# Moving the gate multiplication of a fused attention and mixture kernel from one phase to the input of the next

## The chip, the cores and the metric

One core of one Trainium2 chip runs the whole program in one launch. The metric is the device time of one execution in microseconds (us); lower is better. Engine names are those of the profile: PE is TensorE (its matmuls), PEld its weight loads, DVE is VectorE, ACT is ScalarE, POOL is GpSimd, SP is the engine that only issues transfers here. A queue name with a q (ACTq, SPq) is the instruction stream of an engine as an issuer of transfers.

## The reference

Three layers in a row, in 32-bit floats, for 8 batches of 576 tokens and a model width of 512:

```python
kv  = einsum('bhsd,bhse->bhde', k, v);  out = einsum('bhsd,bhde->bhse', q, kv)   # linear attention, 8 heads of 64
x   = out / sqrt(mean(out^2) + 1e-6) * g_norm
xk, xr = mu_k*x + (1-mu_k)*x_prev,  mu_r*x + (1-mu_r)*x_prev                     # x_prev: one token earlier
v   = relu(xk @ w_k)^2 @ w_v                                                     # 512 -> 1024 -> 512
r   = sigmoid(xr @ w_r)
x2  = r * v                                                                      # the gate multiplication
# then, with x2: 4 experts of causal softmax attention (64 wide), the 2 best of 4 by a router, w_o
```

## The kernel before

All matrices are kept transposed: 128 partitions hold features, the free dimension holds tokens. A 32-bit product is made of three single-pass matmuls: each operand is split into a high part (an ACT copy with rounding) and a low part (a subtraction on DVE or POOL), and `mm3` (lines 74 to 78) adds high by high, high by low and low by high. `split` (lines 70 to 72) is the pair of instructions.

**Stages.** `phase_a` computes the attention, r and relu(.)^2 for all batches; it stores r to the DRAM tensors `sgd` and the squares to `kkd`. `phase_v` (the w_v phase, lines 663 to 760) does the product with w_v, batch by batch, by a seven-product block scheme (`BLOCKS`); the two outer halves of a batch's input (tile `kin`) are subtracted from each other (tiles `tv`, two buffers) and split (tiles `kk`, five buffers) by `prep` (lines 150 to 179), one batch ahead of the products. `phase2` (lines 761 to 1084) does the expert attention.

**The gate in the w_v phase.** `load_s` (lines 144 to 148) loads a batch's r from `sgd` into tiles `sgv`. `gated` (lines 688 to 692) takes one finished quarter: DVE adds or subtracts two terms into a tile `ct` (three buffers), and POOL multiplies `ct` into `sgv` in place. There are eight quarters of 128 x 288 a batch. Two stores on the SP queue (lines 717 and 728) send the gated half batches to the DRAM tensors `x2d`.

**Second-phase weights.** `weights2` (lines 80 to 123) loads and splits the weights of the second phase while the w_v phase runs. The first 256 columns of `w_qk` are scaled by -1/8: a DVE instruction scales the staged tile `wst` in place (line 101), then `split` runs over all 512 columns.

**Second-phase input.** In the second phase a batch has two halves `HF`, tokens 0 to 255 and 256 to 575. `prep(b, hf)` (lines 772 to 787) loads x2 of one half into the tile `x2in` (one buffer, issued on the ACT queue, line 779) and then, in four pieces, rounds it on ACT (line 785) and subtracts on POOL (line 786). For batch 0 it is different: in the last w_v batch (lines 739 to 755) both halves of batch 0 are loaded, and the first half is split there, a piece at a time, between the products; the second half is split at the start of the second phase, with two of its four subtractions on DVE.

**Order of work.** The second phase is software-pipelined by steps `g`: scores, exponentials (`expo`, line 912), normalization on POOL (`norm`, line 929) one step later, transposes on PE (`transp`, line 949) four steps later. There are 18 steps a batch. The next batch's two `prep` generators start at steps `P0` and `P1` and advance by one piece a step; projections of the next batch (`fill_n`) are spread from step `CUT` on. The instructions are written in this order, but outside phase_a a planner (`schedule_with_timeline_sim=True`) sets the order on each engine from its own simulated times: an instruction that is ready in the simulation may go ahead of others written before it on the same engine. `tc.keep_in_program_order` ties an instruction behind the one written before it on its engine. On the chip each engine then runs its list strictly in order, and an instruction that waits holds up all behind it.

Two PSUM tiles `acc` (`AB = 2`) are shared by all projections of the second phase, so the third projection can't start before the first one has been copied out by ACT and DVE.

Of the kernel before, what the change touches and what calls it, by code (L numbers as in the profile page):

```python
# [9 lines left out]
F32 = mybir.dt.float32  # L10
F32R = mybir.dt.float32r
# [4 lines left out]
ALU = mybir.AluOpType  # L16
# [9 lines left out]
def tile_kernel(ctx: ExitStack, tc: tile.TileContext, qT, kv, par, w_r, w_k, w_v, w_qk, w_vg, w_o, out):  # L26
# [53 lines left out]
    def weights2():  # L80
# [16 lines left out]
        def load_w(wh, wl, w, kt, f, scaled=0):  # L97
            st = w2.tile([P, DM], F32, name="wst", bufs=2)
            nc.sync.dma_start(st[:, :f], w[kt * P:(kt + 1) * P, :])
            if scaled:  # L100
                nc.vector.tensor_scalar(st[:, :scaled], st[:, :scaled], -D ** -0.5, None, op0=ALU.mult)
            split(wh[:, kt, :], wl[:, kt, :], st[:, :f])

# [30 lines left out]

    kin, ops, sgt = {}, {}, {}

    def load(b):
        if b < B:
            for h in range(2):
                for i in range(2):  # L140
                    kin[b, i, h] = W["sv"].tile([P, KH, HS], F32, name="kin", bufs=5)
                    nc.sync.dma_start(kin[b, i, h], kkd[b][:, KH * i:KH * i + KH, h * HS:(h + 1) * HS])

    def load_s(b):
        if b < B:
            for i in range(2):
                sgt[b, i] = W["sv"].tile([P, KD // 2, S], F32, name="sgv", bufs=3)
                nc.sync.dma_start(sgt[b, i], sgd[b][:, 2 * i:2 * i + 2, :])

# [513 lines left out]
    def phase_v():  # L663
        with ExitStack():
            sb = W["sv"]

            def products(b):
# [19 lines left out]

                def gated(i, m, h, op, x, y):
                    c = sb.tile([P, HS], F32, name="ct", bufs=3)
                    op(c, x, y)  # L690
                    g = sgt[b, i][:, m, h * HS:(h + 1) * HS]
                    nc.gpsimd.tensor_mul(g, c, g)  # L692
                add, sub = nc.vector.tensor_add, nc.vector.tensor_sub
# [6 lines left out]
                for m in MM:  # L700
                    q = bank()
                    prod(q, "a12", "b21", m, True, True)
                    gated(0, m, 0, add, q[:, :HS], p1[m])
                yield
# [9 lines left out]
                for m in MM:  # L714
                    prod(qd[m], "s4", "b22", m, False, True)
                    gated(0, m, 1, add, qd[m][:, :HS], u2[m])
                nc.sync.dma_start(x2d[b][:, :2, :], sgt[b, 0])
                yield
# [4 lines left out]
                for m in MM:  # L723
                    prod(qa[m], "s3", "t3", m, False, True)
                    u3 = kept(qa[m], "vu")
                    gated(1, m, 1, add, qa[m][:, :HS], p5[m])
                    gated(1, m, 0, sub, u3, qc[m][:, :HS])
                nc.sync.dma_start(x2d[b][:, 2:, :], sgt[b, 1])
                yield

            load_s(0)
            load(1)
            for b in range(B):
                if b > 0:
                    load(b + 1)
                load_s(b + 1)
                if b == 2:
                    w2 = weights2()
                if b == B - 1:
                    for _ in w2:  # L740
                        pass
                    W["x2"] = ExitStack()
                    x2p = W["x2"].enter_context(tc.tile_pool(name="x2p", bufs=1, reuse_waits="tile"))
                    x21 = W["x21"] = x2p.tile([P, KD, S - 256], F32, name="x21")
                    x2, xh, xl = W["x20"] = [x2p.tile([P, KD, 256], t, name=f"x20{u}") for t, u in ((F32, "i"), (F32R, "h"), (F32R, "l"))]
                    nc.sync.dma_start(x2, x2d[0][:, :, :256])
                    nc.sync.dma_start(x21, x2d[0][:, :, 256:])
                pr = prep(b + 1) if b + 1 < B else None
                for n, _ in enumerate(products(b)):
# [3 lines left out]
                    if b == B - 1 and 0 < n < 5:  # L753
                        nc.scalar.activation(xh[:, n - 1, :], x2[:, n - 1, :], AF.Copy)
                        nc.gpsimd.tensor_sub(xl[:, n - 1, :], x2[:, n - 1, :], xh[:, n - 1, :].bitcast(F32))
                for _ in pr or ():
# [4 lines left out]
    def phase2():  # L761
        with ExitStack() as st2:
# [9 lines left out]
            def prep(b, hf):  # L772
                q0, q1 = HF[hf]
                w = q1 - q0
                if b == 0:
                    x2 = W["x21"]
                else:
                    x2 = sb.tile([P, KD, HW], F32, name="x2in", bufs=1)
                    nc.scalar.dma_start(x2[:, :, :w], x2d[b][:, :, q0:q1])
                xh = sb.tile([P, KD, w], F32R, name=f"x2h{hf}", bufs=1)  # L780
# [3 lines left out]
                for i in range(KD):  # L784
                    nc.scalar.activation(xh[:, i, :], x2[:, i, :w], AF.Copy)
                    (nc.gpsimd if b or i % 2 else nc.vector).tensor_sub(xl[:, i, :], x2[:, i, :w], xh[:, i, :].bitcast(F32))  # L786
                    yield
# [227 lines left out]

            x2t[0, 0] = W["x20"][1:]
            for _ in prep(0, 1):
                pass
            for f in fill_n(0):
# [4 lines left out]
            Z0, Z1 = 9, 11  # L1024
            P0, P1 = 3, 9
            L1, L2, L3, L4, L5, L6 = 2, 8, 9, 22, 13, 22
# [32 lines left out]
            for g in range(NG + 2 * NC):  # L1059
                b, s = divmod(g, NS)  # L1060
                if b + 1 < B:
                    if s == P0 + (b == 0):
                        pn = prep(b + 1, 0)
                    if s == P1:
                        pn = prep(b + 1, 1)
                    next(pn, None)
# [61 lines left out]
```

## Time and profile before

| | |
|---|---|
| median of 3 runs | 991.35 us (990.33 to 991.79) |
| the profiled execution's own time | 991.67 us |
| its span (first to last instruction) | 989.9 us |
| mean granted clock of PE | 0.989 of full |
| PE busy | 949.4 us (96%) |
| PEld busy | 870.1 us (88%) |
| DVE busy | 651.5 us (66%) |
| ACT busy | 536.3 us (54%) |
| POOL busy | 427.0 us (43%) |

Read it so: the stages follow each other in time on all engines. phase_a runs to about 390 us, the w_v phase from there to 604 us, the second phase from 604 us to the end. A busy share of PE near 100% in a stretch means that matmuls follow each other without a gap that the profile shows; only a stretch below that has time to give back. The time of an execution is 1.8 us more than its span.

### The profile page before, as it was taken

To read this page: it belongs to the slowest core of one execution; us is meant where nothing else is said; L and a number is where in the kernel's file an instruction comes from. 1 tells how busy PE (TensorE), PEld (TensorE's weight loads), DVE (VectorE), ACT (ScalarE), POOL (GpSimd) and SP (SyncE) were. 2 spreads that over 40 slices of the span, in tenths; PEclk is the share of its full clock that TensorE was granted. 3 is DMA by queue.
4 is the path that set the end of the run, shared out by engine and by line. 5 is a ranking of instruction groups with operands and counts; after the bars stand their busy time and mean duration, and the time that the engine had idled before them with its cause. 6 is when DMAs were issued, how large, how long until landed. Compare 5 with 4: busy or idle time off the path is not lost.

```text
span 989.9 us, 20990 instructions
## 1 busy us (share of the span) xinstructions
PE 949.4 (96%) x7912; PEld 870.1 (88%) x7912; DVE 651.5 (66%) x1537; ACT 536.3 (54%) x1320; POOL 427.0 (43%) x516
## 2 busy tenths in 40 slices
PE   5779999999999999999999998999999999999998
PEld 2669899989899999999999997988988888888986
DVE  4897675867576763579987883665556565656553
ACT  4664765756666665455454543546354546455454
POOL 0025052433253422657888885427152433435231
PEclk9789999999999999999999999999999999999999
DMA  9752737363546224866666623002030202120102
GB/s 345 228 162 91 226 106 237 110 222 123 199 147 196 74 79 117 294 196 223 220 217 210 208 104 116 22 6 97 1 97 2 96 27 71 28 71 27 49 13 85
DMA packets 74901, 127.20 MB, mean 129 GB/s; under 512 B 6448, under 2 KB 57136, under 8 KB 74800
## 3 DMA queue, kind: packets, MB, share of 16 engines
q1 hardware_dynamic: 57760, 104.10, 31.4%
q10 hardware_dynamic: 17040, 21.77, 7.0%
q8 instruction: 62, 1.02, 0.4%
q14 instruction: 39, 0.32, 0.1%
HBM read 78.66 MB, written 47.19 MB: 127 GB/s over the span
## 4 chain that ended last, share of the span: by engine, by line
PE 76%; DVE 7%; ACT 7%; DMA 5%; POOL 3%; issue 2%; ACTq 0%; DVEq 0%; POOLq 0%
PE acc L76 16%; PE acc L77 15%; PE acc L78 15%; PE qa L680 6%; PE qd L680 4%; PE acc L680 4%; DMA x2in<-x2d 3%; PE acc L976 3%; PE pt L949 3%; PE s L900 2%; ACT pr L912 2%; POOL x2l L786 2%; PE acc L300 2%; POOL pr L929 1%; PE po L316 1%
## 5 line engine op out<-in xcount | busy, mean ns | idle before, releaser
L437 POOL TENSOR_TENSOR ksq<-rl 128x288 f32<-128x288 f32 x128 | 99.5, 783 | 148.2 <-ACT rl L435 142.7
L77 PE MATMUL acc<-mixl,wkh 128*128 128x288 f32 x512 | 154.3, 302 | 0.2 <-DVE mixl L66 0.2
L76 PE MATMUL acc<-mixh,wkh 128*128 128x288 f32 x512 | 151.1, 299 | 3.4 <-ACT mixh L409 2.8
L78 PE MATMUL acc<-mixh,wkl 128*128 128x288 f32 x512 | 151.3, 296 | 0.0
L912 ACT ACTIVATE pr<-pr,nm 128x256 f32<-128x256 f32 (+4 forms) x144 | 83.2, 579 | 73.3 <-DVE nm L866 72.4
L929 POOL TENSOR_SCALAR pr<-pr,rc,wg 128x512 f32<-128x512 f32 (+3 forms) x128 | 76.2, 608 | 104.0 <-DVE wg L859 62.4
L76 PEld LDWEIGHTS acc<-mixh,wkh 128*128 128x128 f32 x512 | 96.3, 190 | 4.6 <-ACT mixh L409 3.3
L77 PEld LDWEIGHTS acc<-mixl,wkh 128*128 128x128 f32 x512 | 97.1, 190 | 2.2 <-DVE mixl L66 0.4
L692 POOL TENSOR_TENSOR sgv<-ct,sgv 128x288 f32<-128x288 f32 x64 | 82.5, 1313 | 35.2 <-DVE ct L690 34.7
L78 PEld LDWEIGHTS acc<-mixh,wkl 128*128 128x128 f32 x512 | 97.4, 190 | 0.0
L403 DVE TENSOR_TENSOR mixl<-xm,mixh 128x288 fp32r<-128x288 f32 x116 | 58.3, 538 | 52.3 <-ACT mixh L409 52.3
L435 ACT ACTIVATE rl<-acc 128x288 f32<-128x288 f32 x128 | 51.6, 405 | 71.5 <-PE acc L78 52.7
L866 DVE CUSTOM_DVE_ANT_0 pr<-s,mask 128x256 f32<-128x256 f32 (+4 forms) x144 | 66.9, 481 | 17.2 <-PE pt L949 12.8
L76 PE MATMUL acc<-x2h,wqh 128*128 128x320 f32 (+1 forms) x240 | 74.5, 311 | 3.5 <-DVE vs L829 3.5
L76 PE MATMUL acc<-mixh,wrh 128*128 128x288 f32 x240 | 74.6, 311 | 0.6 <-ACT sg L66 0.6
L408 DVE SCALAR_TENSOR_TENSOR xm<-xT,pars,xm 128x288 f32<-128x288 f32 x116 | 69.0, 624 | 5.1 <-ACT xm L400 5.0
L78 PE MATMUL acc<-x2h,wql 128*128 128x320 f32 (+1 forms) x240 | 71.2, 297 | 0.0
L400 ACT ACTIVATE xm<-xT,nus 128x288 f32<-128x288 f32 x120 | 61.0, 532 | 18.8 <-DVE mixl L403 9.2
L77 PE MATMUL acc<-x2l,wqh 128*128 128x320 f32 (+1 forms) x240 | 71.1, 296 | 0.0
L78 PE MATMUL acc<-mixh,wrl 128*128 128x288 f32 x240 | 71.0, 296 | 0.0
L77 PE MATMUL acc<-mixl,wrh 128*128 128x288 f32 x240 | 70.4, 293 | 0.0
L72 DVE TENSOR_TENSOR kk<-tv,kk 128x1152 fp32r<-128x1152 f32 x32 | 59.8, 1886 | 7.3 <-ACT kk L71 7.3
(239 smaller groups left out, 2753.4 us busy)
## 6 DMA issues: line engine op xcount, KB each, us to landing
kkd<-ksq SPq DMA_DIRECT2D x128, 144.0 KB, 1.8
kin<-kkd SPq DMA_DIRECT2D x32, 576.0 KB, 4.6
kvt<-in_kv SPq DMA_DIRECT2D x24, 512.0 KB, 5.7
qt<-in_qT SPq DMA_DIRECT2D x16, 576.0 KB, 7.0
sgv<-sgd SPq DMA_DIRECT2D x16, 576.0 KB, 3.8
x2d<-sgv SPq DMA_DIRECT2D x16, 576.0 KB, 2.9
sgd<-sg ACTq DMA_DIRECT2D x56, 144.0 KB, 3.7
out<-ob SPq DMA_DIRECT2D x28, 288.0 KB, 2.1
```

The costliest lines, as they stand in the source:

```text
L72: vec.tensor_sub(lo, src, hi.bitcast(F32))
L76: ten.matmul(ps, wh(i), xh(i), start=(i == 0), stop=False)
L77: ten.matmul(ps, wh(i), xl(i), start=False, stop=False)
L78: ten.matmul(ps, wl(i), xh(i), start=False, stop=(i == n - 1))
L400: act.activation(xs[p], xT[:, p, h * HS:(h + 1) * HS], AF.Copy, scale=nu[:, p:p + 1])
L408: vec.scalar_tensor_tensor(xs[p], xT[:, p, cols(h)], mu[:, p:p + 1], xs[p], op0=ALU.mult, op1=ALU.add)
L437: nc.gpsimd.tensor_mul(sq, rl, rl)
L680: nc.tensor.matmul(q[:, :HS], a[:, i, ms_], c[:, i, :], start=(start and i == 0 and n == 0), stop=(stop and i == KH - 1 and n == 2), skip_ ...
L692: nc.gpsimd.tensor_mul(g, c, g)
L866: nc.vector.tensor_tensor_reduce(out=pr[:R, k0:k0 + kn], in0=s[:R, :kn], in1=mk, scale=1.0, scalar=lo, op0=ALU.add, op1=ALU.min, accum_out ...
L912: nc.scalar.activation(pr[:, :L], pr[:, :L], AF.Exp, bias=nm, scale=-1.0, accum_out=sms[b, p, j][:, e2:e2 + 1])
L929: nc.gpsimd.tensor_scalar(pr[:, :L], pr[:, :L], rc[:, r:r + 1], wg, op0=ALU.mult, op1=ALU.mult)
```

## The change

- `gated` becomes `put`: DVE writes each finished quarter straight into an output tile `vo` (three buffers of a half batch); the POOL multiplication, the tile `ct` and the loads of `sgd` in the w_v phase go. `x2d` then holds v, not r * v.
- In the last w_v batch both halves of batch 0 are loaded in four parts, each with its part of r; the loads reuse the buffers `kin` and `tv`. After each of the products 1 to 4, one part is multiplied on POOL, rounded on ACT and subtracted on POOL. The second phase starts with batch 0 split whole.
- `prep` of the second phase loads x2 and r (tile `gin`), two buffers each, on the SP queue. Each piece is multiplied on POOL in place, rounded on ACT (now tied in program order) and subtracted on POOL.
- `P1` is 8 and not 9, and what is left of the first half's generator is run out before the second starts.
- The scaled columns of `w_qk` are rounded by ACT with the scale inside, and DVE makes the low part in one instruction with the scale inside.

```diff
         def load_w(wh, wl, w, kt, f, scaled=0):
...
             if scaled:
-                nc.vector.tensor_scalar(st[:, :scaled], st[:, :scaled], -D ** -0.5, None, op0=ALU.mult)
-            split(wh[:, kt, :], wl[:, kt, :], st[:, :f])
+                nc.scalar.activation(h[:, :scaled], st[:, :scaled], AF.Copy, scale=-D ** -0.5)
+                nc.vector.scalar_tensor_tensor(l[:, :scaled], st[:, :scaled], -D ** -0.5, h[:, :scaled].bitcast(F32), op0=ALU.mult, op1=ALU.subtract)
+            split(h[:, scaled:], l[:, scaled:], st[:, scaled:f])
...
-                def gated(i, m, h, op, x, y):
-                    c = sb.tile([P, HS], F32, name="ct", bufs=3)
-                    op(c, x, y)
-                    g = sgt[b, i][:, m, h * HS:(h + 1) * HS]
-                    nc.gpsimd.tensor_mul(g, c, g)
+                out_ = [sb.tile([P, KD // 2, S], F32, name="vo", bufs=3) for _ in range(2)]
+
+                def put(i, m, h, op, x, y):
+                    op(out_[i][:, m, h * HS:(h + 1) * HS], x, y)
...
-                nc.sync.dma_start(x2d[b][:, :2, :], sgt[b, 0])
+                nc.sync.dma_start(x2d[b][:, :2, :], out_[0])
...
-                load_s(b + 1)
...
-                    x21 = W["x21"] = x2p.tile([P, KD, S - 256], F32, name="x21")
-                    x2, xh, xl = W["x20"] = [x2p.tile([P, KD, 256], t, name=f"x20{u}") for t, u in ((F32, "i"), (F32R, "h"), (F32R, "l"))]
-                    nc.sync.dma_start(x2, x2d[0][:, :, :256])
-                    nc.sync.dma_start(x21, x2d[0][:, :, 256:])
+                    cuts = [(0, 256), (256, S)]
+                    W["x2t"] = [[x2p.tile([P, KD, c1 - c0], F32R, name=f"x2{i}{u}") for u in "hl"] for i, (c0, c1) in enumerate(cuts)]
+                    parts = []
+                    for (c0, c1), hl in zip(cuts, W["x2t"]):
+                        for i in range(0, KD, 2):
+                            raw = []
+                            for name, src, n in (("kin", x2d, 5), ("tv", sgd, 2)):
+                                t = sb.tile([P, KH, HS], F32, name=name, bufs=n).rearrange("p k t -> p (k t)")[:, :2 * (c1 - c0)]
+                                raw.append(t.rearrange("p (k t) -> p k t", k=2))
+                                nc.sync.dma_start(raw[-1], src[0][:, i:i + 2, c0:c1])
+                            parts.append([x[:, i:i + 2, :] for x in hl] + raw)
...
                     if b == B - 1 and 0 < n < 5:
-                        nc.scalar.activation(xh[:, n - 1, :], x2[:, n - 1, :], AF.Copy)
-                        nc.gpsimd.tensor_sub(xl[:, n - 1, :], x2[:, n - 1, :], xh[:, n - 1, :].bitcast(F32))
+                        h, l, x, g = parts[n - 1]
+                        nc.gpsimd.tensor_mul(x, x, g)
+                        act.activation(h, x, AF.Copy)
+                        nc.gpsimd.tensor_sub(l, x, h.bitcast(F32))
...
-                if b == 0:
-                    x2 = W["x21"]
-                else:
-                    x2 = sb.tile([P, KD, HW], F32, name="x2in", bufs=1)
-                    nc.scalar.dma_start(x2[:, :, :w], x2d[b][:, :, q0:q1])
+                x2, g = [sb.tile([P, KD, HW], F32, name=name, bufs=2) for name in ("x2in", "gin")]
+                for t, src in ((x2, x2d), (g, sgd)):
+                    nc.sync.dma_start(t[:, :, :w], src[b][:, :, q0:q1])
...
-                    nc.scalar.activation(xh[:, i, :], x2[:, i, :w], AF.Copy)
-                    (nc.gpsimd if b or i % 2 else nc.vector).tensor_sub(xl[:, i, :], x2[:, i, :w], xh[:, i, :].bitcast(F32))
+                    x = x2[:, i, :w]
+                    nc.gpsimd.tensor_mul(x, x, g[:, i, :w])
+                    tc.keep_in_program_order(nc.scalar.activation(xh[:, i, :], x, AF.Copy))
+                    nc.gpsimd.tensor_sub(xl[:, i, :], x, xh[:, i, :].bitcast(F32))
...
-            for _ in prep(0, 1):
-                pass
...
-            P0, P1 = 3, 9
+            P0, P1 = 3, 8
...
                     if s == P1:
+                        for _ in pn:
+                            pass
                         pn = prep(b + 1, 1)
```

## Rows read from the trace of the kernel before

**Rows 1.** Stretches: start:end, length, busy PE PEld DVE ACT POOL, PEclk, DMA, GB/s.
```profile
440.00:450.00 10.00, 8.49 (x64) 8.20 (x63) 10.00 (x10) 4.66 (x10) 8.45 (x4) 1.00 0.69 199
...
480.00:600.00 120.00, 120.00 (x892) 118.78 (x891) 99.14 (x89) 54.00 (x76) 95.77 (x55) 1.00 0.55 184
...
615.00:625.00 10.00, 6.53 (x39) 6.36 (x40) 2.28 (x9) 3.90 (x11) 0.74 (x3) 0.83 0.23 67
...
650.00:930.00 280.00, 276.06 (x2228) 244.96 (x2228) 165.17 (x619) 145.53 (x454) 114.94 (x190) 1.00 0.15 50
```

**Rows 2.** Waits of PE, whole span: waiter <- releaser: us in total, times, longest.
```profile
PE acc L76 <- DVE vs L829: 3.5, 1, 3.5
PE qa L680 <- DVE ct L690: 3.2, 2, 1.7
...
PE acc L76 <- ACT yh L71: 2.1, 4, 0.6
...
PE acc L76 <- ACT ob L999: 1.0, 6, 0.2
...
PE acc L76 <- DVE qs L72: 0.8, 1, 0.8
```

**Rows 3.** POOL groups, 390 to 607 us: busy, mean ns | idle before.
```profile
L692 POOL TENSOR_TENSOR sgv<-ct,sgv 128x288 f32<-128x288 f32 x64 | 82.5, 1313 | 35.2 <-DVE ct L690 34.7 <-DVE tri L121 0.4
```

**Rows 4.** Line L72, 390 to 600 us: duration ns min/median/max, first and last start.
```profile
L72 DVE TENSOR_TENSOR kk<-kin,kk x24: 1343/1958/3862, 400.4 to 583.4; 128x1152 fp32r<-128x1152 f32 x24
```

**Rows 5.** Timeline of DVE, 440 to 452 us: start, length, what [idle before].
```profile
440.10 2.77 DVE L101 TENSOR_SCALAR wst<-wst 128x256 f32<-128x256 f32 x1
...
449.38 0.45 DVE L690 TENSOR_TENSOR ct<-qa,vq 128x288 f32<-128x288 f32 x1
```

**Rows 6.** Timeline of ACT, 595 to 640 us.
```profile
606.85 0.60 ACTq L779 DMA_DIRECT2D x2in<-x2d  x1
611.80 1.34 ACT L785 ACTIVATE x2h<-x2in 128x256 fp32r<-128x256 f32 x4 [4.62 <-DMA x2in<-x2d]
615.19 0.53 ACTq L779 DMA_DIRECT2D x2in<-x2d  x1
615.75 1.28 ACT L912 ACT_TABLE_LOAD   x1 [2.61 <-POOL x2l L786]
```

**Rows 7.** Timeline of DVE, 598 to 645 us.
```profile
605.22 1.97 DVE L786 TENSOR_TENSOR x2l<-x,x2h 128x320 fp32r<-128x320 f32 x2
...
612.43 0.08 DVE L866 DVE_READ_ACCUMULATOR2_ANT nm<- 128x1 f32 x1
...
617.96 0.17 DVE L922 TENSOR_SCALAR sm<-sm 128x2 f32<-128x2 f32 x1 [5.09 <-ACT pr L912]
618.03 0.42 DVE L829 COPY vs<-acc 128x260 f32<-128x260 f32 x1
```

**Rows 8.** Timeline of ACT, 700 to 760 us (the third steady batch).
```profile
724.22 1.55 ACT L785 ACTIVATE x2h<-x2in 128x320 fp32r<-128x320 f32 x4 [1.30 <-DMA x2in<-x2d]
725.68 0.36 ACT L71 ACTIVATE yh<-acc 128x256 fp32r<-128x256 f32 x1
```

**Rows 9.** Timeline of POOL, 700 to 760 us.
```profile
724.78 3.37 POOL L786 TENSOR_TENSOR x2l<-x2in,x2h 128x320 fp32r<-128x320 f32 x4 [1.20 <-ACT x2h L785]
728.12 0.86 POOL L929 TENSOR_SCALAR pr<-pr,rc,wl 128x576 f32<-128x576 f32 x1
```

**Rows 10.** Timeline of PE, 724 to 732 us.
```profile
729.03 0.77 PE L949 MATMUL pt<-ident,pr 128*128 128x128 f32 x5
```

**Rows 11.** Instructions of line L786, whole span.
```profile
L786 POOL TENSOR_TENSOR x2l<-x2in,x2h x56: 717/804/894, 612.3 to 913.4; 128x256 fp32r<-128x256 f32 x28, 128x320 fp32r<-128x320 f32 x28
```

**Rows 12.** Instructions of line L922, whole span.
```profile
L922 DVE TENSOR_SCALAR sm<-sm x80: 141/169/1536, 618.0 to 971.4; 128x2 f32<-128x2 f32 x64, 128x1 f32<-128x1 f32 x16
```

**Rows 13.** DMA issues by line: KB each, median us from issue to landing.
```profile
x2in<-x2d ACTq DMA_DIRECT2D x7, 640.0 KB, 4.3
```

**Rows 14.** Timeline of DVE, 580 to 605 us.
```profile
590.99 3.46 DVE L72 TENSOR_TENSOR kk<-tv,kk 128x1152 fp32r<-128x1152 f32 x2
```

More of the change, by code (lines that the diff above doesn't have):

```diff
@@ L99, in load_w @@
             nc.sync.dma_start(st[:, :f], w[kt * P:(kt + 1) * P, :])
+            h, l = wh[:, kt, :], wl[:, kt, :]
             if scaled:
-                nc.vector.tensor_scalar(st[:, :scaled], st[:, :scaled], -D ** -0.5, None, op0=ALU.mult)
-            split(wh[:, kt, :], wl[:, kt, :], st[:, :f])
+                nc.scalar.activation(h[:, :scaled], st[:, :scaled], AF.Copy, scale=-D ** -0.5)
+                nc.vector.scalar_tensor_tensor(l[:, :scaled], st[:, :scaled], -D ** -0.5, h[:, :scaled].bitcast(F32), op0=ALU.mult, op1=ALU.subtract)
+            split(h[:, scaled:], l[:, scaled:], st[:, scaled:f])
         yield
@@ L133, in tile_kernel @@
     blk = {}
-    kin, ops, sgt = {}, {}, {}
+    kin, ops = {}, {}
     def load(b):
@@ L142, in load @@
                     nc.sync.dma_start(kin[b, i, h], kkd[b][:, KH * i:KH * i + KH, h * HS:(h + 1) * HS])
[L144 to L148, printed above, removed]
     def prep(b):
@@ L702, in products @@
                     prod(q, "a12", "b21", m, True, True)
-                    gated(0, m, 0, add, q[:, :HS], p1[m])
+                    put(0, m, 0, add, q[:, :HS], p1[m])
                 yield
@@ L715, in products @@
                     prod(qd[m], "s4", "b22", m, False, True)
-                    gated(0, m, 1, add, qd[m][:, :HS], u2[m])
-                nc.sync.dma_start(x2d[b][:, :2, :], sgt[b, 0])
+                    put(0, m, 1, add, qd[m][:, :HS], u2[m])
+                nc.sync.dma_start(x2d[b][:, :2, :], out_[0])
                 yield
@@ L725, in products @@
                     u3 = kept(qa[m], "vu")
-                    gated(1, m, 1, add, qa[m][:, :HS], p5[m])
-                    gated(1, m, 0, sub, u3, qc[m][:, :HS])
-                nc.sync.dma_start(x2d[b][:, 2:, :], sgt[b, 1])
+                    put(1, m, 1, add, qa[m][:, :HS], p5[m])
+                    put(1, m, 0, sub, u3, qc[m][:, :HS])
+                nc.sync.dma_start(x2d[b][:, 2:, :], out_[1])
                 yield
-            load_s(0)
             load(1)
@@ L1014, in fill_o @@
                 return [lambda m=m, hf=hf: wo_group(b, hf, m) for hf, m in (sorted(order) if b == B - 1 else order)]
-            x2t[0, 0] = W["x20"][1:]
-            for _ in prep(0, 1):
-                pass
+            x2t[0, 0], x2t[0, 1] = W["x2t"]
             for f in fill_n(0):
```

## The prediction

> **What bounds the kernel now.** I read the page's busy shares first, then the busy time by stretches, then what PE waited for, and last the timelines around each wait. The stretches show that the w_v phase and the second phase are bound by PE: it is busy for 120.00 of 120.00 us between 480 and 600 us, and for 276.06 of 280 us between 650 and 930 us [rows 1]. No matmul is added or removed by the change. So an engine that gets less to do gives nothing by itself, and the time can fall only by what PE now waits. I take about 0.2%, 2 us, as what a measurement of this kernel can tell from no change.
>
> PE's waits in the reach of the change are few. In the w_v phase it waits 3.2 us in two pieces for DVE's `ct`, the first of which shows in the stretch from 440 us as 8.49 us busy of 10 [rows 1, 2]. At the start of the second phase it waits 0.8 us for a query split on DVE and 3.5 us, in one piece, for the copy of a value tile on DVE [rows 2]. In the steady batches it waits 2.1 us in four pieces for `yh` and 1.0 us in six for `ob`, both from ACT [rows 2]. Behind the 3.5 us there is a second cost: the stretch from 615 to 625 us has a mean granted clock of 0.83 [rows 1]. The clock has two levels, 2.4 GHz and half of it, so 3.4 of the 10 us were at the lower one, and 1.7 us of PE work was lost there. All this is 3.2 + 0.8 + 3.5 + 1.7 + 2.1 + 1.0 = 12.3 us. It is the ceiling of the gain, unless the planner's new order also opens gaps that are not listed as waits.
>
> **The w_v phase.** Removed: 64 POOL multiplications of 1.313 us mean, 82.5 us of POOL [rows 3], and 16 loads of `sgd`. PE didn't wait for POOL, so this is worth nothing directly. What it frees is DVE. A split of 128 x 1152 takes DVE 1.343 us at best and 1.958 us in the median [rows 4]; 56 of them (seven a batch) at 0.6 us too much are 34 us. In the stretch from 440 us, where PE waits first, DVE is busy for 10.00 of 10 us [rows 1]; behind a scaling of `wst` that took 2.77 us, it comes to the `ct` that PE waits for only at 449.38 us [rows 5]. The scaling goes (four instructions), ACT gets one more rounding instruction in each of the four weight tiles, and DVE's 512-wide subtraction becomes two of 256. Thus DVE gets less work in just the stretch where it is late. Both pieces should go. But POOL keeps its sixteen differences of 128 x 1152, and DVE its other splits of weights, so I leave a little: between 0 and 3.2 us, taken as 3.0.
>
> Why the splits stretch can be read in the Trainium skill (SBUF — State Buffer, Who interferes with whom): DVE and POOL share one pair of ports as an exclusive lock, and a DVE instruction with two SBUF inputs blocks against a POOL instruction that reads SBUF. The trace agrees as far as 1.343 against 1.958 us goes [rows 4]. By that rule the splits fall back towards 1.34 us wherever no difference runs, and the sum is the same.
>
> `put` adds a wait on the `vo` buffers: with three of them, a half batch reuses a buffer whose store was issued at least half a batch before. I cost this at nothing; a store that was late would hold DVE, and PE behind it.
>
> **Batch 0's input.** Four parts are loaded, multiplied, rounded and subtracted in the last w_v batch. The work on POOL is 2 x 4 instructions of 512 or 640 columns: at 0.717 to 0.894 us for 256 to 320 columns [rows 11] and twice the width, about 8 x 1.6 = 13 us. The removed multiplications of that batch make the room. The loads can't start early: they take turns on the two `tv` buffers, behind the last two splits of `tv`, which run from 590.99 to 594.45 us [rows 14]. From there, with loads of about 4 us [rows 13] and parts in pairs on two buffers: the first half is ready at about 600 us, the second at about 606 us. PE starts the second phase at 604 us with the first half and needs the second at about 611 us. So it is hidden with 4 to 5 us to spare; each us beyond that would be a us of PE, and a long wait brings the low clock again.
>
> **The start of the second phase.** The chain behind the 3.5 us: the planner put the load of batch 1 on ACT's queue at 606.85 us and its rounding at once behind it; ACT stood for 4.62 us until the load landed, then the issue of the second load stood for another 2.61 us until POOL had freed the single `x2in` buffer, and only at 615.75 us came the first exponential's table load [rows 6]. DVE's `sm` waited for that until 617.96 us and held the copy of `vs` behind it, for which PE waited [rows 7]. All three causes go: the loads are on SP, there are two buffers, and the rounding is tied behind the exponentials of step 3. The scores are ready at 612.5 us (the last maximum is read at 612.43 us [rows 7]), so table load and first exponential end at 612.5 + 1.28 + 0.9 = 614.7 us instead of 617.96. The copy of `vs` then ends at about 615.1 us; PE came to it at 618.45 - 3.5 = 615.0 us (it ended at 618.03 + 0.42). The wait and the slow clock after it nearly vanish. The 0.8 us goes too: DVE was then on its two subtractions of batch 0's second half (1.97 us from 605.22 us [rows 7]), which are gone. Of 0.8 + 3.5 + 1.7 = 6.0 us I leave 0.7 us, half a table load, for the in-order chain that stays: 5.3 us.
>
> **The steady batches.** Removed from ACT: 14 issues of 0.53 to 0.60 us [rows 6] and the wait for the landing, such as 1.30 us before the rounding at 724.22 us; `yh`, for which PE waits, stands right behind it [rows 8]. With two buffers a load is issued as soon as the half before the last is split, some ten steps ahead of use, so it should land in time although there are twice as many. I count the 2.1 us of `yh` as gone and leave `ob`. On SP a load may wait for its buffer; behind it stand only the output stores, and their four `ob` tiles have a batch of time.
>
> Added to POOL: 7 batches x 8 multiplications, 56 x 0.804 = 45 us, sized by the subtractions of the same shape [rows 11]. POOL was busy for 114.94 of 280 us [rows 1], so it has room; its share goes to about 55%. The cost to PE lies between 0 and 45 us. The nearest row is the 56 subtractions themselves: none of PE's waits names POOL [rows 2], though the margin can be small (the normalization at 728.12 ends at 728.98 us, behind four subtractions, and its transposes start at 729.03 us [rows 9, 10]). A multiplication is ready long before its rounding and fills idle time, so I take 0.6 us in all. Net for this stage: 2.1 - 0.6 = 1.5 us.
>
> Sum: 3.0 + 5.3 + 1.5 = 9.8 us. The profiled execution took 991.67 us (span 989.9), 0.3 us over the median of the runs shown. 991.67 - 9.8 = 981.9; I say 982.
>
> **Rivals.**
> 1. *The start stays slow.* The new order there is the planner's, and DVE still holds `vs` behind `sm`, so another late exponential gives another PE wait with its slow clock. For: the margin computed above is about zero. Against: 7.2 us of ACT's standing is gone. Gains 3.0 + 0.8 + 1.5 = 5.3: 986.4.
> 2. *POOL becomes the late one (slower).* The 8 multiplications of a batch stand in bursts ahead of normalizations, as the subtractions do at 724.78 us [rows 9]. For: the 0.05 us margin [rows 9, 10], and SP loads that land later on the chip than planned would hold POOL's list. Against: normalizations are earlier in the program and go first when ready. If one burst of four multiplications (3.4 us) is exposed in each of 7 batches: + 24; 991.67 - 3.0 - 5.3 + 24 = 1007; with half of it exposed, 995. It is slower than before from 9.8 / 7 = 1.4 us a batch on.
> 3. *Little moves.* PE was full in the w_v phase anyway, and both small waits there and the start are replaced by others as long (DVE still has the differences, batch 0's parts come late): about 990.
> 4. *All waits go*, `ob` too: 991.67 - 12.3 = 979.4.
>
> For the second rival a rule of the Trainium skill (the same page and section) speaks as well: the new multiplications hold the port pair against DVE's small scalings, and the trace has `sm` at 0.169 us in the median and 1.536 us at most [rows 12]; by that rule each multiplication could cost DVE up to 0.8 us, while most of DVE's work there has one input in PSUM and would not be touched.
>
> **Chances.** The forecast 0.50, rival 1 0.20, rival 2 0.10, rival 3 0.10, rival 4 0.10. The range reaches from the ceiling of the gain with some room for a better order (977) to rival 3 (990); it holds all but most of rival 2 and the ends of the others. Faster by over 0.2% (below 989.4): the forecast, rivals 1 and 4 and a third of rival 3, 0.83; within 0.2%: 0.07; slower (over 993.3): 0.10.
>
> **What would show it.** In the changed profile: (a) no wait of PE for an instruction of the quarter additions in the w_v phase, and splits with a median near 1.4 us; (b) between 604 and 625 us no PE wait above 1 us and a granted clock of 1.00; (c) no ACT wait for a load in the second phase, and `yh` gone from PE's waits; (d) POOL's normalization not named in PE's waits. The prediction is wrong if PE waits for batch 0's second half near 611 us, if POOL or a transfer into `x2in` or `gin` heads PE's waits, or if the time lies above 990.

## The result and the profile after

| | before | after |
|---|---|---|
| median | 991.57 us (990.33 to 992.18, 4 runs) | 979.43 us (978.65 to 980.26, 4 runs) |
| ratio | | 0.988, 95% interval 0.9865 to 0.9896 |
| profiled execution | 991.67 us | 979.24 us, span 977.5 us |

The change is faster by 1.2%. The forecast was 982.0 us; the time is inside the range and 2.6 us below the forecast, at the number of the fourth rival.

The stretches of the kernel after, in the columns of [rows 1]:

```profile
440.00:450.00 10.00, 8.17 (x59) 7.70 (x58) 9.63 (x10) 4.05 (x8) 5.35 (x2) 1.00 0.56 173
460.00:480.00 20.00, 20.00 (x153) 20.00 (x152) 17.93 (x18) 9.56 (x14) 5.36 (x2) 1.00 0.58 179
480.00:600.00 120.00, 120.00 (x904) 120.00 (x904) 88.51 (x86) 56.81 (x80) 37.12 (x18) 1.00 0.47 149
615.00:625.00 10.00, 8.71 (x67) 7.92 (x66) 7.37 (x27) 3.85 (x13) 6.56 (x12) 1.00 0.31 96
650.00:920.00 270.00, 269.10 (x2172) 237.63 (x2172) 159.67 (x601) 143.75 (x445) 142.89 (x225) 1.00 0.22 68
```

From 615 to 625 us the granted clock is 1.00 where it was 0.83, and PE does 67 matmuls where it did 39 [rows 1]. Between 480 and 600 us POOL falls from 95.77 to 37.12 us; PE is called busy for all 120 us in both, and yet starts 904 matmuls where it started 892. So a busy share of 100% can still hide time: 12 matmuls at 120 / 904 = 0.133 us are 1.6 us. It isn't true, then, that only a stretch with a lower share has time to give back, as the text on the profile before has it. A matmul there lasts about 0.3 us in the profile and the next one starts 0.133 us behind it, so a pause of a tenth of a us leaves no idle time on PE. It does show on PE's weight loads: PEld was busy for 118.78 of the 120 us before [rows 1] and is for 120.00 after, and before, it waited there four times for a split on DVE:

```profile
PEld acc L680 <- DVE kk L72: 0.8, 4, 0.2
```

After, no row of waits of PEld is left in that stretch. The stretch from 460 to 480 us has 16 matmuls more than this one of the kernel before:

```profile
460.00:480.00 20.00, 18.30 (x137) 18.06 (x137) 18.43 (x17) 10.47 (x18) 18.00 (x12) 1.00 0.62 204
```

The rest of the profile after: PE's waits that answer to [rows 2] (the largest in the reach of the change, `vs`, `yh` and `ob` are no longer among them), the splits of [rows 4], and ACT's timeline at the start of the second phase, to be held against [rows 6].

```profile
PE qa L676 <- DVE vo L687: 1.8, 2, 1.2
PE acc L76 <- DVE qs L72: 1.3, 1, 1.3
...
PE acc L978 <- DVE pt L962: 0.9, 1, 0.9
```

```profile
L72 DVE TENSOR_TENSOR kk<-kin,kk x24: 1346/1358/3381, 399.8 to 579.7; 128x1152 fp32r<-128x1152 f32 x24
```

```profile
603.91 1.28 ACT L914 ACT_TABLE_LOAD   x1
607.62 0.40 ACT L914 ACTIVATE pr<-pr,nm 128x128 f32<-128x128 f32 x1 [2.43 <-DVE nm L868]
```

The table load comes at 603.91 us, long before it is needed, and the first exponential waits for its maximum and not for a transfer.

To see where the 12.4 us between the two spans went, I cut each trace at PE's milestones: the second phase's first matmul, and the first attention-value matmul of each batch. These two lines of the kernel before, and the two after, bound the five steady batches:

```profile
697.17 0.49 PE L976 MATMUL acc<-pt,vs 128*64 128x320 f32 x2
...
929.76 0.49 PE L976 MATMUL acc<-pt,vs 128*64 128x320 f32 x2
```

```profile
687.81 0.49 PE L978 MATMUL acc<-pt,vs 128*64 128x320 f32 x2
...
917.75 0.49 PE L978 MATMUL acc<-pt,vs 128*64 128x320 f32 x2
```

That is 232.6 against 229.9 us. "w_v" runs from PE's 2001st matmul with `mixh` or `mixl` (the tiles of `phase_a`'s projections) to the second phase, and "start" from there to the first of the two lines, so it holds the whole first batch:

| kernel (profiled execution) | w_v, us | start | steady, a batch | span |
|---|---|---|---|---|
| before | 224.7 | 93.4 | 46.52 | 989.9 |
| after | 222.1 | 87.3 | 45.99 | 977.5 |
| v_gate_off | 225.2 | 92.9 | 46.6 | 989.0 |
| loads_only | 224.8 | 87.1 | 45.6 | 978.0 |
| lo_one_buffer | 224.8 | 87.6 | 46.8 | 987.1 |
| lo_act_queue | 224.8 | 87.3 | 45.4 | 977.4 |
| lo_no_tie | 224.9 | 89.1 | 45.4 | 978.6 |
| act_queue | 223.4 | 90.3 | 46.8 | 985.8 |
| no_mul2 | 223.3 | 86.0 | 45.65 | 975.5 |
| old_scale | 222.8 | 87.1 | 46.0 | 977.9 |
| loads_weights | 230.0 | 87.0 | 45.6 | 983.1 |
| loads_scale | 228.9 | 87.0 | 45.4 | 981.8 |
| loads_scale_batch0 | 231.1 | 86.0 | 45.5 | 983.0 |
| tie_one | 221.8 | 88.0 | 46.7 | 981.0 |

The 12.4 us are 2.6 in w_v, 6.1 at the start, 2.65 in the five steady batches, 0.4 behind them, and 0.7 in `phase_a`, whose code is the same. Each row is one execution. Up to that 2001st matmul they differ by as much as 1.4 us (377.7 to 379.1), and lo_one_buffer comes to it only at 380.9 us. Behind it they agree better: w_v is 224.7 to 224.9 us in the five kernels that have the same order of work there (before, loads_only and the three lo_ kernels), and the five batches of loads_only take 45.60 to 45.63 us each. So a tenth or two in one row show nothing.

### The profile page after: what moved, and what is told of

It reads as the page before. It is cut to its first block, busy times and chain, and to the rows that moved or that the text cites. A ratio compares the mean times of both kernels' runs of the same rounds, so it can differ in the third digit from the quotient of the medians.

```text
span 977.5 us, 20974 instructions
## 1 busy us (share of the span) xinstructions
PE 944.1 (97%) x7912; PEld 866.8 (89%) x7912; DVE 635.1 (65%) x1535; ACT 538.2 (55%) x1320; POOL 382.5 (39%) x510
## 4 chain that ended last, share of the span: by engine, by line
PE 82%; DVE 7%; ACT 5%; DMA 3%; issue 2%; POOL 1%; ACTq 0%; SPq 0%; POOLq 0%; DVEq 0%
PE acc L76 16%; PE acc L77 16%; PE acc L78 15%; PE qa L676 7%; PE acc L978 5%; PE qd L676 4%; PE pt L951 4%; PE acc L676 4%; PE s L902 3%; PE acc L296 2%; PE s L887 1%; PE po L312 1%; PE acc L66 1%; ACT pr L914 1%; DMA kkd<-ksq 1%
## 5 line engine op out<-in xcount | busy, mean ns | idle before, releaser
L433 POOL TENSOR_TENSOR ksq<-rl 128x288 f32<-128x288 f32 x128 | 101.9, 803 | 150.1 <-ACT rl L431 144.9
L76 PE MATMUL acc<-x2h,wqh 128*128 128x256 f32 (+1 forms) x224 | 69.5, 310 | 0.0
L72 DVE TENSOR_TENSOR kk<-tv,kk 128x1152 fp32r<-128x1152 f32 x32 | 51.4, 1607 | 27.2 <-ACT kk L71 27.1
L77 PE MATMUL acc<-x2l,wqh 128*128 128x256 f32 (+1 forms) x224 | 66.1, 295 | 0.0
L78 PE MATMUL acc<-x2h,wql 128*128 128x256 f32 (+1 forms) x224 | 66.1, 295 | 0.0
L951 PE MATMUL pt<-ident,pr 128*128 128x128 f32 x400 | 63.4, 277 | 0.6
```

The lines of the kernel that those rows point to most:

```text
L76: ten.matmul(ps, wh(i), xh(i), start=(i == 0), stop=False)
L77: ten.matmul(ps, wh(i), xl(i), start=False, stop=False)
L78: ten.matmul(ps, wl(i), xh(i), start=False, stop=(i == n - 1))
L433: nc.gpsimd.tensor_mul(sq, rl, rl)
L951: nc.tensor.transpose(pt[:, (i - i0) * P:(i - i0 + 1) * P], pr[:, k1 - P:k1], ident)
```

## The experiments

**v_gate_off: the w_v part alone, on the kernel before.** The multiplication by r is left out altogether, so POOL has it nowhere, and r isn't loaded.

```diff
                 def gated(i, m, h, op, x, y):
-                    c = sb.tile([P, HS], F32, name="ct", bufs=3)
-                    op(c, x, y)
-                    g = sgt[b, i][:, m, h * HS:(h + 1) * HS]
-                    nc.gpsimd.tensor_mul(g, c, g)
+                    op(out_[i][:, m, h * HS:(h + 1) * HS], x, y)
```

> The kernel before with the gate multiplication left out altogether (the quarters go straight into the output tile, r is not loaded; the result is v, not r * v); loads, buffers and batch 0 of the second phase as before. Theory 1 (three separate gains: the w_v phase 3.3 us, the start of the second phase about 6 us, the steady batches about 2.7 us): only the first is had, about 988.2 us, the start keeps its 3.5 us wait, and the splits of 128 x 1152 fall from a median of 1.96 to about 1.36 us. Rival (POOL's work in the w_v phase was hidden, and the later start of the second phase is moved by it as well): 991.5 us if hidden, or under 985 us if the start depends on it.

Measured: 990.34 us, ratio 0.9984 (0.9974 to 0.9993): 1.6 us in 991.7, between the two expected times. The stretches of its profiled execution (990.73 us):

```profile
440.00:450.00 10.00, 6.94 (x44) 6.71 (x43) 9.63 (x10) 4.81 (x8) 5.86 (x2) 0.81 0.47 148
460.00:480.00 20.00, 20.00 (x152) 20.00 (x151) 16.45 (x17) 12.31 (x20) 11.36 (x6) 1.00 0.55 166
480.00:600.00 120.00, 120.00 (x904) 120.00 (x903) 91.90 (x88) 54.81 (x78) 28.36 (x16) 1.00 0.43 139
```

One instruction of its DVE timeline, the one of POOL beside it, and the wait that ends on PE's:

```profile
442.74 2.98 DVE L72 TENSOR_TENSOR wql<-wst,wqh 128x512 fp32r<-128x512 f32 x1
```

```profile
441.97 3.20 POOL L159 TENSOR_TENSOR tv<-tv,kin 128x1152 f32<-128x1152 f32 x1 [11.86 <-DMA x2d<-vo]
```

```profile
447.40 0.85 PE L680 MATMUL qa<-kk,wh_a 128*128 128x288 f32 x2 [3.06 <-DVE vo L691]
```

The later stretches have the 904 and 152 matmuls: the gate's leaving is worth 1.6 + 15 x 0.133 = 3.6 us there. All of it is lost again from 440 us on, where PE waits 3.06 us in one piece and then has a mean granted clock of 0.81. Ahead of that wait DVE has a split of second-phase weights that takes 2.98 us. So the gate's leaving frees DVE as predicted, and by itself gives PE next to nothing.

**loads_only: three lines on the kernel before.** Two `x2in` buffers, issued on SP, the rounding tied. The gate stays in the w_v phase.

```diff
-                    x2 = sb.tile([P, KD, HW], F32, name="x2in", bufs=1)
-                    nc.scalar.dma_start(x2[:, :, :w], x2d[b][:, :, q0:q1])
+                    x2 = sb.tile([P, KD, HW], F32, name="x2in", bufs=2)
+                    nc.sync.dma_start(x2[:, :, :w], x2d[b][:, :, q0:q1])
...
-                    nc.scalar.activation(xh[:, i, :], x2[:, i, :w], AF.Copy)
+                    ro = nc.scalar.activation(xh[:, i, :], x2[:, i, :w], AF.Copy)
+                    if b:
+                        tc.keep_in_program_order(ro)
```

> The kernel before with the second phase's loads alone changed: on the SP queue, two buffers, rounding tied in program order for batches 1 to 7; the gate stays in the w_v phase and batch 0's second half is still split at the start of the second phase. Theory 1: the start and the steady batches gain almost as in the changed kernel, about 5.2 + 2.7 us, so 983.5 us, with no 3.5 us wait and no low clock. Rival (the start is won by having batch 0 split whole before it): the start keeps most of its wait, about 988.5 us.

Measured: 980.18 us, 0.9883 (0.9869 to 0.9898), the same as the whole change and 3.3 us less than expected. The start is 6.3 us shorter and each batch 0.9 us, and w_v is as before. Of PE's waits between 390 and 960 us only these are over 0.3 us; `vs`, `yh` and `ob` are gone:

```profile
PE qa L680 <- DVE ct L690: 3.2, 2, 1.7
PE acc L76 <- DVE qs L72: 1.7, 2, 0.8
```

**act_queue: the changed kernel with both loads on ACT's queue and one buffer each.**

```diff
-                x2, g = [sb.tile([P, KD, HW], F32, name=name, bufs=2) for name in ("x2in", "gin")]
+                x2, g = [sb.tile([P, KD, HW], F32, name=name, bufs=1) for name in ("x2in", "gin")]
...
-                    nc.sync.dma_start(t[:, :, :w], src[b][:, :, q0:q1])
+                    nc.scalar.dma_start(t[:, :, :w], src[b][:, :, q0:q1])
```

> The changed kernel with both loads of the second phase on ACT's queue and one buffer each. Theory 1: the start's wait and the steady batches' waits come back, 987 to 988 us, and ACT again waits for landings. Rival (batch 0 split whole, not the loads, won the start): about 982 us, the steady batches alone slower.

Measured: 986.92 us, 0.995 (0.9935 to 0.9965): 7.5 us of the gain go. The next runs part the two edits.

**no_mul2: the changed kernel without the 56 multiplications of batches 1 to 7** (their gate is left out; the loads of r stay).

```diff
-                    nc.gpsimd.tensor_mul(x, x, g[:, i, :w])
```

> The changed kernel without the 56 multiplications of the second phase (batches 1 to 7 go in without the gate; r is still loaded). It prices the added POOL work. Theory 1 (hidden work): 979.4 us within 0.6 us. Rival (POOL's multiplications hold up normalizations or DVE's small instructions): 3 us or more faster.

Measured: 977.48 us, 0.9856 (0.9841 to 0.987), 2.0 us below the changed kernel. A batch takes 45.65 in place of 45.99 us, the start 86.0 in place of 87.3.

**lo_one_buffer, lo_act_queue, lo_no_tie: loads_only less one of its three lines each.**

```diff
-                    x2 = sb.tile([P, KD, HW], F32, name="x2in", bufs=2)
+                    x2 = sb.tile([P, KD, HW], F32, name="x2in", bufs=1)
```

> loads_only (980.2 us: the kernel before with the second phase's loads on SP, two buffers, rounding tied) with one buffer again. Theory A (what cost time was ACT's standing at the issue of a load, behind a transfer or a buffer; SP can stand instead without harm): the start stays quick and a batch stays at 45.6 us, 980.5 us within 1. Theory B (the late landing itself, due to the single buffer): a batch goes back to 46.5 us and the start loses some us, 986 us or more.

```diff
-                    nc.sync.dma_start(x2[:, :, :w], x2d[b][:, :, q0:q1])
+                    nc.scalar.dma_start(x2[:, :, :w], x2d[b][:, :, q0:q1])
```

> loads_only with the loads on ACT's queue again, two buffers and the tie kept. Theory A: an issue waits for no transfer at the start with two buffers and the tie, so the start stays quick; each issue costs ACT 0.5 us, and where its buffer is not free yet ACT stands: 981 to 983 us, a batch of 45.6 to 46.0. Theory B (the queue is what counts): 987 us or more.

```diff
-                    if b:
-                        tc.keep_in_program_order(ro)
```

> loads_only without the tie of the rounding in program order. Theory A' (the tie is what clears the start: without it the planner puts the rounding of batch 1 ahead of the first exponentials, where ACT stands for the landing): the start's wait of PE comes back in part, about 2 to 4 us with its slow clock, 983 to 986 us, batches stay at 45.6 us. Theory C (the queue and the buffers clear the start): 980.2 us within 0.8.

Measured: one buffer 986.11 us (0.9956, 0.994 to 0.9973), ACT's queue 979.46 (0.9884, 0.9869 to 0.9899), no tie 980.7 (0.9896, 0.9881 to 0.991). With two buffers the queue is worth nothing. With one buffer the batches are at least as long as before, and PE waits again for what ACT does late. PE's largest wait, and who waited for `x2in`, in that kernel:

```profile
PE acc L76 <- ACT ob L1001: 5.6, 5, 1.6
```

```profile
  ACT x2h L785: 7.3, 7
```

Those 7.3 us are ACT's waits for landings, one for each of seven loads; the single buffer came free too late, whichever queue stood for it. With two buffers neither row is there. At the start one buffer does little harm as long as SP issues (87.6 us); with one buffer on ACT's queue (act_queue) the start is 90.3 us. Without the tie the start is 2.0 us longer and the batches 0.2 us shorter. ACT without the tie:

```profile
610.90 1.34 ACT L785 ACTIVATE x2h<-x2in 128x256 fp32r<-128x256 f32 x4 [4.86 <-DMA x2in<-x2d]
612.26 1.28 ACT L912 ACT_TABLE_LOAD   x1
```

The rounding goes ahead of the table load again and stands 4.86 us for the landing, as in [rows 6]; only the second stand, 2.61 us for the buffer, is gone.

**old_scale: the changed kernel with the old weight scaling.**

```diff
-                nc.scalar.activation(h[:, :scaled], st[:, :scaled], AF.Copy, scale=-D ** -0.5)
-                nc.vector.scalar_tensor_tensor(l[:, :scaled], st[:, :scaled], -D ** -0.5, h[:, :scaled].bitcast(F32), op0=ALU.mult, op1=ALU.subtract)
-            split(h[:, scaled:], l[:, scaled:], st[:, scaled:f])
+                nc.vector.tensor_scalar(st[:, :scaled], st[:, :scaled], -D ** -0.5, None, op0=ALU.mult)
+            split(h, l, st[:, :f])
```

> The changed kernel with the scaling of the query weights as before (DVE scales the staged tile in place, then one split over 512 columns). Theory D (the w_v phase gained by the weights' edit, not by the gate's leaving): the w_v phase grows by 1 to 2.5 us and PE's wait for the quarter additions is 3 us again, 981 us. Theory E (it gained by the gate's leaving): 979.4 us within 0.6.

Measured: 979.56 us, 0.9881 (0.9864 to 0.9897): no difference in time from the changed kernel, as theory E said. In its profile, though, w_v is 0.7 us longer (222.8 against 222.1), and PE's wait for the quarter additions is nearly as long as theory D said:

```profile
PE qa L675 <- DVE vo L686: 2.8, 2, 1.5
```

So the runs show that the scaling is worth less than they can tell, not that it is worth nothing.

**loads_weights, loads_scale, loads_scale_batch0: more of the change on top of loads_only, the gate still in the w_v phase.** The first adds the new scaling with all the weights' roundings tied; the second the new scaling untied, and ties the input's rounding for batch 1 alone; the third adds batch 0's whole split to the second.

```diff
+            pin(nc.scalar.activation(h[:, scaled:], st[:, scaled:f], AF.Copy))
...
-                    if b:
+                    if b == 1:
                         tc.keep_in_program_order(ro)
...
+                        h, l, x = parts[n - 1]
+                        act.activation(h, x, AF.Copy)
+                        nc.gpsimd.tensor_sub(l, x, h.bitcast(F32))
```

> loads_only with two edits of the second-phase weights: the scale inside the rounding and the low part, as in the changed kernel, and each rounding on ACT tied in program order, so that the weights are spread over batches 2 to 6 of the w_v phase and not bunched at 430 to 470 us. The gate stays in the w_v phase. If PE's 3.2 us there come from the bunched weights: both waits go, 977 us, faster than both kernels. If they come from the gate's multiplications on POOL: 980 us.

> loads_only with the scale inside the rounding of the weights, as in the changed kernel, and the tie of the rounding for batch 1 alone; the gate stays in the w_v phase. Theory D: the w_v phase is 1 to 2.5 us shorter than in loads_only; a steady batch takes 45.4 us as without the tie; so 977 us. Theory E: only the 1 us of the tie, 979 us.

> loads_scale with both halves of batch 0 loaded and split in the last w_v batch as in the changed kernel (without a multiplication, as the gate is still in the w_v phase). What it should take away is PE's 1.0 us wait for DVE's query split at the start and DVE's two subtractions: 1 us less than loads_scale, about 976 us. If POOL's gate multiplications hold the four parts up, PE waits near the first value group of the second half, and it is slower than loads_scale.

Measured: 985.11 us (0.9941, 0.9924 to 0.9957), 978.22 (0.9882, 0.9855 to 0.9909) and 983.21 (0.9923, 0.9909 to 0.9938). The start and the batches came out as expected (86.0 us with batch 0 whole, 1.0 less), but in the three profiled executions w_v is 4 to 6 us longer than in loads_only. In that of loads_scale (983.54 us, where its other three took 977.84 to 978.38, so that they can hardly have lost this time) PE's wait for the quarter additions and the stretch around it are:

```profile
PE qa L682 <- DVE ct L692: 6.2, 7, 4.0
```

```profile
460.00:480.00 20.00, 15.97 (x109) 15.73 (x108) 16.54 (x16) 8.95 (x15) 16.73 (x12) 0.91 0.61 200
```

One wait of 4.0 us, then a lower mean clock: 153 - 109 = 44 matmuls, 5.8 us, fewer than after. For loads_weights neither of the expected times came. loads_scale lies between its two, so it doesn't tell whether the scaling is worth something. loads_scale_batch0 is slower than loads_scale, but not by the wait that was expected: PE waits 2.8 us in one piece inside w_v, for a copy by ACT. So batch 0's whole split gains 1.0 us at the start and loses more than that in w_v: with the gate still on POOL, the kernel is 5.0 us slower for it. That the gate's leaving makes room for it in the changed kernel is likely, but not shown. None of these kernels beats the change by more than can be measured.

**tie_one: the changed kernel with the tie for batch 1 alone.**

```diff
-                    tc.keep_in_program_order(nc.scalar.activation(xh[:, i, :], x, AF.Copy))
+                    rounded = nc.scalar.activation(xh[:, i, :], x, AF.Copy)
+                    if b == 1:
+                        tc.keep_in_program_order(rounded)
```

> The changed kernel, with the rounding of the next batch's input tied in program order only for batch 1 (as in the first second-phase batch) and free for batches 2 to 7. Theory F (tie pays only at the start: without it the start was 2.0 us longer, but each steady batch 0.2 us shorter): the start stays at 87.3 us, the batches fall from 46.0 to about 45.8 us, and the time is 1.0 to 1.4 us less than the changed kernel's: about 978.2. Rival: with the multiplications on POOL the rounding has to wait for them, and free in the planner's order it goes ahead of exponentials again and stands before them: batches of 46.2 us or more, 980.5 or later. Neither: 979.4, no difference that can be measured.

Measured: 982.37 us, 0.9911 (0.9894 to 0.9927), 2.9 us more than the changed kernel. The steady batches take 46.6, 46.6, 49.35, 45.4 and 45.5 us. Theory F is wrong for the first three of them, where the rival (46.2 us or more) came true: with the multiplications on POOL the order of work matters more than in lo_no_tie. The one of 49.35 us in the timelines of DVE, POOL and PE:

```profile
812.67 4.75 DVE L926 TENSOR_SCALAR sm<-sm 128x2 f32<-128x2 f32 x1
```

```profile
812.41 0.81 POOL L933 TENSOR_SCALAR pr<-pr,rc,wl 128x576 f32<-128x576 f32 x1
813.21 0.87 POOL L933 TENSOR_SCALAR pr<-pr,rc,wg 128x128 f32<-128x128 f32 x2
814.06 3.33 POOL L786 TENSOR_TENSOR x2in<-x2in,gin 128x320 f32<-128x320 f32 x4
```

```profile
818.35 0.30 PE L953 MATMUL pt<-ident,pr 128*128 128x128 f32 x1 [2.00 <-DVE pt L964]
```

The stretch behind that wait:

```profile
820.00:829.50 9.50, 9.50 (x67) 9.42 (x67) 3.41 (x16) 3.95 (x11) 3.42 (x5) 0.84 0.40 133
```

A DVE instruction on 128 x 2 numbers, 0.169 us in the median [rows 12], starts at 812.67 us beside a run of POOL instructions without a gap; they end at 814.06 + 3.33 = 817.39 us, and it ends at 817.42 us. PE waits 2.0 us, and 0.16 of the clock over 9.5 us are another 1.5 us.

## Why the prediction was right, and where it was not

**The start (5.3 predicted, 6.1 measured): right, by the chain it gave.** The runs take it apart: second buffer on SP 4.3 us (93.4 to 89.1), the tie 2.0 (to 87.1), batch 0 whole 1.0 (loads_scale to loads_scale_batch0), less 1.3 for the multiplications (no_mul2 against after). The three causes are not a sum: with the tie and SP the second buffer is worth only 0.5 us (lo_one_buffer), with the tie and the buffer SP is worth 0.2 (lo_act_queue); ACT's second stand goes by either. The wait that stays, 1.3 us for `qs`, is of the kind that the 0.7 us were left for. Sign (b) missed its bound of 1 us by that wait and held for the clock. Batch 0's input came earlier than the 606 us of the prediction: its last subtraction ends at 597.88 + 3.10 = 600.98 us.

```profile
597.88 3.10 POOL L757 TENSOR_TENSOR x21l<-kin,x21h 128x640 fp32r<-128x640 f32 x2
```

The wait for a `vo` buffer, costed at nothing, doesn't show either: none of DVE's idle time ahead of `vo` ends with a store.

**The steady batches (1.5 predicted, 2.65 measured): the mis-sized terms.** The prediction counted the 2.1 us of `yh` as gone and left `ob`. In loads_only the five batches give 232.6 - 228.0 = 4.6 us. The prediction read the waits of PE's matmuls alone; those of its weight loads are longer. In the five batches of the kernel before:

```profile
PEld acc L76 <- ACT yh L71: 4.0, 5, 0.9
PEld acc L76 <- ACT ob L999: 2.1, 5, 0.4
```

In those of loads_only `yh` is gone, and of `ob` this is left:

```profile
PEld acc L76 <- ACT ob L1001: 1.2, 5, 0.2
```

That is 4.0 + 0.9 = 4.9 us less, about the 4.6. The multiplications on POOL were set at 0.6 us in all; loads_only to after is 45.6 to 45.99, some 0.35 to 0.4 us a batch, about 2 us over five batches, and 1.3 at the start. So the two terms are 4.6 and -1.9, not 2.1 and -0.6. Sign (c) held: ACT waits for no load, since POOL's multiplication now does that waiting, where PE doesn't see it. The idle time ahead of the instructions on `x2in` in the kernel after:

```profile
  DMA x2in<-x2d: 9.1, 5
```

Sign (d) held.

**The w_v phase (3.0 predicted, 2.6 measured): the size right, half of the cause wrong.** The step "DVE gets less work in just the stretch where it is late. Both pieces should go" failed for the first piece. The splits did fall to 1.358 us [against rows 4], and the second piece, in the stretch from 460 us, went with them (16 x 0.133 = 2.1 us). The first stayed: from 440 to 450 us PE does 59 matmuls where it did 64. The scaling that the prediction blamed is gone, but DVE is as late as before, in two splits of weights of 128 x 260 beside one of POOL's differences, which stay:

```profile
440.12 3.27 DVE L72 TENSOR_TENSOR wgl<-wst,wgh 128x260 fp32r<-128x260 f32 x2 [0.18 <-ACT wgh L71]
```

```profile
440.07 2.68 POOL L155 TENSOR_TENSOR tv<-tv,kin 128x1152 f32<-128x1152 f32 x1 [10.82 <-DMA wst<-in_w_vg]
```

The shortest of these splits takes 0.416 us, so 2.4 of the 3.27 us are extra. With the old scaling (old_scale) the time is the same. In place of the first piece came 1.6 us that the prediction had no term for, 12 more matmuls in a stretch that was already 100% busy; half of them stood in the waits of the weight loads, which it didn't read. So sign (a) is half right: the median fell, a wait of 1.8 us stays.

The gate's leaving is thus worth about 3.6 us, as v_gate_off shows from 460 us on, and a single wait ahead of that decides how much of it the kernel keeps: against the kernel before, the changed kernel loses 5 matmuls between 440 and 450 us, v_gate_off 20. In part that is luck. no_mul2 and act_queue have the same code in the w_v phase as the changed kernel, and there the planner put one DVE split a place earlier; their w_v takes 223.3 and 223.4 us in place of 222.1, with a wait that the changed kernel doesn't have. In no_mul2:

```profile
PE qd L676 <- ACT vq L681: 1.3, 1, 1.3
```

So the phase gains 1.3 to 2.6 us. How the planner's order comes to place the weight splits better in one kernel than in the other was not taken apart: v_gate_off and the changed kernel both lack the gate there, and they differ in batch 0's input, the loads and the scaling, of which only the scaling was tried by itself. The edit of `P1` was not tried by itself either.

**The rivals.** The fourth has the right number by sums that are partly others: its ceiling of 12.3 us was built from listed waits, and a w_v wait, `qs` and `pt` stay, while 1.6 us in w_v and more than its rows listed in the steady batches went. That it hits the measured number is luck. The first was tried in lo_no_tie: 2.0 us, not 4.5. The second, POOL late, did not come in this order of work but lies close: tie_one frees one kind of instruction and has it once, for 3.5 us. There the prediction's "up to 0.8 us" for each multiplication was too small, since the short DVE instruction lost a whole run of POOL instructions. The Trainium skill (SBUF — State Buffer, Who interferes with whom) says of a DVE instruction in a mode with two ports, which `tensor_scalar` can enter, that it or the GpSimd instruction, whichever issues first, holds the shared ports for its whole length and the other fully blocks. The 4.75 us agree with a full block, but they span more than one POOL instruction, which the section doesn't say; no run shows the mode that this one was in.

Of what the change is named for, the gate's move and batch 0's split, the first brings 1.3 to 2.6 us in w_v and takes back about 3.2 us behind it, the second brings 1.0. What pays are the second buffer and the tie that came with them; loads_only has the whole gain.

## What to carry to other kernels

A load that is waited for in an engine's in-order list needs its second buffer first: here that one line is worth about 1 us of each 46.5 us batch, and with it the queue that issues the load is worth nothing. Relief of an engine that PE waits for only now and then is paid out only if the one wait that remains doesn't grow: in the profiled execution of v_gate_off a wait of 3.06 us, with the low clock behind it, took back all that the later stretches gained. Read the waits of PE's weight loads beside those of its matmuls, and compare the number of matmuls in fixed stretches of two traces: both show time that PE's busy share and its own waits don't.

## What the runs showed of the hardware

- A DVE `tensor_scalar` of 128 x 2 took 4.75 us in place of 0.169 beside a gapless run of seven POOL instructions, and ended 0.03 us after them (tie_one).
- A DVE subtraction of 128 x 512 with two inputs took 2.98 us beside a POOL difference of 3.20 us, where its fellows took 0.68 us in the same kernel (v_gate_off).
- PE waits of 3.06 and 4.0 us were each followed by a lower mean granted clock (0.81 over 10 us in v_gate_off, 0.91 over 20 us in loads_scale), and so was one of 2.0 us (0.84 over 9.5 us in tie_one), while in the kernel before the two `ct` waits of 1.7 us or less left the clock at 1.00 [rows 1, 2].
